# Giving the first weighted group of an attention + expert-mixture kernel the same matmul scheme as the others, with a new order where the scheme begins

## The chip, the cores and the metric

The kernel runs on one core of a Trainium2 chip. The metric is the device time of one execution in microseconds, as the median of several. Engines are named as in the profile: PE is TensorE, DVE VectorE, ACT ScalarE, POOL GpSimd, SP SyncE, which here only issues DMAs.

## The reference

Two blocks follow one another. The first is attention with a polynomial sketch in place of the softmax, for 4 x 4 heads of 1088 positions and 32 dimensions. Its output, read as 4352 rows of 128, is `x` of the second, a mixture of eight experts in which every expert sees every row and a Sinkhorn iteration gives the weights:

```python
logits = x @ w_gate                      # x: 4352 x 128, w_gate: 128 x 8
P = np.exp(logits - logits.max())
for _ in range(8):
    P /= P.sum(1, keepdims=True) + 1e-09
    P /= P.sum(0, keepdims=True) + 1e-09
    P *= N / E
for e in range(E):                       # w1[e]: 128 x 1024, w2[e]: 1024 x 128
    out += P[:, e:e + 1] * (np.maximum(x @ w1[e], 0.0) @ w2[e])
```

All of it is float32. Since P is positive, P times relu(x w1) is relu of (P times x) w1, so a kernel may weigh x ahead of an expert, or an expert's sum after it.

## The kernel before

Everything lies transposed: the 4352 rows of x are columns of a tile `xT`, features on the partitions. The expert part is a list of **groups**, each a range of columns with a number of tiles and a list of experts. An **item** is a group with one of its experts. An item's 1024 hidden features are eight slices of 128, and a **block** is half an item (four slices, in groups of three tiles of 256 columns) or a quarter (two slices, in groups of two tiles). A block has **first products**, x times W1, which ACT turns into hidden values by relu, and **second products**, hidden values times W2, which add up over the item or the group in four PSUM banks.

The routing weights are known only after the attention, so the list begins with **plain** groups (last field False): experts 0 and 1 on chosen columns, with unweighted x. Their sums are kept (`kept`) and weighed later. After them come five weighted groups of 768 columns, the first of them (`PLAIN`, columns 1280 to 2047) with experts 1 to 7, and at the end a weighted group of two tiles (columns 0 to 511) with experts 2 to 7. Plain groups run between the pieces of attention and routing.

The second products use fewer multiplications than the plain ones: seven for eight (`seven`) in groups of two tiles, twenty for twenty-four (`twenty`) in groups of three. For that, sums and differences of hidden values are made on DVE (`two`, `sum_of_four`), and sums and differences of W2 (the ten pieces of `make_four` on DVE and two on ACT, kept in DRAM by `store_four` for later groups).

The first products exist in two forms. The **old scheme** (`four`) multiplies as usual: per block 16 matmuls of 128 rows by 64 columns of the array, eight over 512 and eight over 256 columns of x. The **new scheme** (`middle`) has seven products, M1 to M7, in place of eight for a pair of slices, each two matmuls of 64 by 64 over 384 columns, 28 matmuls in a block; a block has two pairs, e and o. It needs W1 in two prepared forms (`forms_ahead`: loads, sign changes on ACT and adding DMAs on POOL's queue, results `wl` and `wf` in DRAM), x in two halves, weighed on DVE (`weigh_half`), copied on ACT (`copy_half`) and joined by four adding DMAs on POOL's queue (`join_halves`), and for each pair six copies and relus and a DVE addition ahead of M3 and one after M7. In that scheme also the second products are split by rows into 64 by 64 matmuls.

All engine orders are written out by hand. In plain groups, and in the old scheme, a loop in `steps` emits a first product, then what is due at that step; second products follow eight steps behind (`LAG`). In the new scheme each operation has a time within a period of 8.83 us, and all operations are sorted by these times and emitted in that order; the times fix only the order. DMAs that `keep_in_program_order` holds stand in their queue (SP's or POOL's) where the program puts them.

The new scheme begins with `first_new`, the third item of the first weighted group, expert 3:

```python
first_weighted = next(j for j, (g, e) in enumerate(items) if g == PLAIN)
first_new = first_weighted + 2
```

Experts 1 and 2 of that group run in the old scheme, with x weighed by POOL (`weigh`) or DVE (`weigh_by_vector`) and with raw W1. During their 32 steps, `beside` and `PREPARE` also make these experts' forms of W2, the W1 forms of expert 1, and the joined x of expert 3. At the seam to the new scheme, the second products of the last two old blocks fill TensorE while the first new blocks start. Routing ends with a transpose on DVE, four DMAs of the weights to `pT` in DRAM, all on SP's queue, and loads of a row of `pT`, repeated over all partitions, to `px`.

Of the kernel before, what the change touches and what calls it, by code (L numbers as in the profile page):

```python
# [10 lines left out]
F32 = mybir.dt.float32  # L11
# [7 lines left out]
def f64_to_f32(nc, pool, raw, shape):  # L19
# [5 lines left out]
    def u32(name):  # L25
        return pool.tile([p, n], U32, name=name)

    def f32(name):
        return pool.tile([p, n], F32, name=name)

    mant, top, expo, rest = u32("mant"), u32("top"), u32("expo"), u32("rest")
    out, inside, over = f32("s12"), f32("inside"), f32("over")
# [18 lines left out]
def kernel(  # L51
# [278 lines left out]

    def projections():
        flat = raw.rearrange("p n d -> p (n d)")
        s12 = f64_to_f32(nc, consts, flat, (P, 2 * D)) if words == 2 else flat.bitcast(F32)
        st = consts.tile([P, 2, 32], F32, name="st")
# [312 lines left out]
    def routing():  # L647
# [4 lines left out]
        for i, e in enumerate(range(items[first_new][1], E)):  # L652
# [46 lines left out]
        for b in (1, 0, 2, 3):  # L699
            nc.sync.dma_start(out=pT[:, b * S:(b + 1) * S],  # L700
                                                  in_=lgT[32 * b:32 * b + E].rearrange("p a s -> p (a s)"))
# [13 lines left out]
              (512, 384, 2, [1], False)]  # L715
# [24 lines left out]
    def prepare_w(j):  # L740
        g, e = items[j]
        three = groups[g][2] == 3
# [5 lines left out]
        else:  # L748
            loaded_w[j] = load_w(e, not three)
            if not three:  # L750
                ws, own = loaded_w[j][2]
                loaded_w[j] = *loaded_w[j][0:2], ws
                sums_ahead[j] = [lambda: weigh_by_vector(j, slice(0, 512)), *own]
        if three:
            loaded_w[j] = *loaded_w[j][0:2], sums_of_four(e)
# [7 lines left out]
    def first_weights(j):  # L763
        e = items[j][1]
        loaded_w[j] = []
        for t, tag in zip(fast[e], ("w1", "w2")):
            w = wpool.tile([P, F], F32, tag=tag, name=tag)
            tc.keep_in_program_order(nc.sync.dma_start(out=w, in_=t))
            loaded_w[j].append(w)
# [6 lines left out]
    def raw_second(j, tag):  # L776
        raw_w2[j] = wpool.tile([P, FO, DM], F32, tag=tag, name=tag)
# [15 lines left out]
    def weigh(out, x, pb):  # L793
        tc.keep_in_program_order(nc.gpsimd.tensor_tensor(out, x, pb, op=Alu.mult))

    def prepare_x(j):
# [5 lines left out]
        else:  # L802
            xe = weights_of(e, lo, t * n, "px")
            for sl in (slice(0, 512), slice(512, 768)) if j == first_weighted else ():
                weigh(xe[:, sl], x[:, sl], xe[:, sl])
            sources[j] = xe
# [36 lines left out]
    first_new = first_weighted + 2  # L843
# [3 lines left out]
    def weigh_kept(g, i, at_, add):  # L847
# [3 lines left out]
        pb = spare[:, (6 + 3 * (i % 2)) * NT3:][:, 0:n * t]  # L851
# [35 lines left out]
    def part(g, k):  # L887
# [4 lines left out]
        elif groups[g][2] == 3:  # L892
# [91 lines left out]
    def evacuate(k):  # L984
        g = ended.pop(k)
        part_of_twenty(g, k)
# [76 lines left out]
    LAG = 8  # L1063
# [4 lines left out]
    def room_of(k):  # L1068
# [8 lines left out]
        one, other = (13 * NT3 + size * ((k + 1) % 3), size * (k % 2)) if weighted else (size * (k % 3), size * (3 + k % 2))  # L1077

        def at(c):
            return base[:, c:c + size].rearrange("p (b n) -> p b n", b=4)[:, :, 0:n]  # L1080
# [58 lines left out]

    def four(k):  # L1140
        j, q = blocks[k]
        h = hs[k] = room_of(k)
        order = ((0, 0), (3, 0), (3, 1), (0, 1), (1, 0), (2, 0), (1, 1), (2, 1))

        def step(c):
            f, last = order[c]
            if last:
                first(k, 4 * q + PLACE[f], 2 * NT3, 3 * NT3, h[:, at(f, 2)], False)
            else:
                first(k, 4 * q + PLACE[f], 0, 2 * NT3, h[:, at(f, 0):at(f, 2)], False)  # L1150

        def sums(c):
            for i in {2: (0,), 3: (1,), 4: (2,), 6: (3, 4), 7: (7, 5), 8: (6,), 9: (8, 9)}.get(c, ()):
                sum_of_four(k, *SUMS[i][1:])

        return 8, step, sums
# [105 lines left out]
    def middle():  # L1262
# [21 lines left out]
        def first_product(k, p, n):  # L1284
# [3 lines left out]
            fa, fb = P * (4 * q + p), P * (4 * q + p + 2)  # L1288
            issued.append(n)
# [3 lines left out]
                      3: (by, 1, w1, fb, de[:, 0], False, True), 4: (b, 1, wf, fb, xe[:, 1], False, True),  # L1293
                      5: (b, p, wf, fa, de[:, 1], True, False), 6: (b, 0, wf, fb, de[:, 0], False, True),
# [20 lines left out]
        def vector(k, p, what):  # L1315
# [7 lines left out]
                  (17.63, 17.59, 19.18, 21.80, 21.41, 23.38, 23.73, 22.41, 24.54, 24.29))  # L1323
        EMPTY = 20.23, 24.2, 24.3, 29.0
        EASE, WEIGH = (11.93, 16.87, 13.85), 13.49

        def whole_product(k, i):
            if k not in products:
                products[k] = twenty(k)
            for p_ in products[k][i]:  # L1330
                into(items[blocks[k][0]][0], *p_)
                written.update({(p_[2], row): -1 for row in range(2)})
# [398 lines left out]
```

## Time and profile before

| | |
|---|---|
| time, median of 3 runs | 888.86 us (888.22 to 889.25) |
| the profiled execution | 889.38 us |
| its span in the profile | 887.6 us |
| PE, DVE, ACT, POOL busy | 99%, 88%, 63%, 19% |
| granted TensorE clock, mean | 0.998 |
| chain that ended last | PE 91%, DVE 4%, DMA 3%, issue 1%, ACT 1% |

All marks in time below are microseconds from the start of the span. A float32 matmul is recorded as two instructions, which overlap with their neighbours; so a record's duration is longer than what it adds to the chain, and costs are better read from the distance of marks and the number of records between. In the lines, `128*64` is the part of the array that a matmul uses, and `x4` the number of instructions merged in a line.

### The profile page before, as it was taken

To read this page: it belongs to the slowest core of one execution; us is meant where nothing else is said; L and a number is where in the kernel's file an instruction comes from. 1 tells how busy PE (TensorE), PEld (TensorE's weight loads), DVE (VectorE), ACT (ScalarE), POOL (GpSimd) and SP (SyncE) were. 2 spreads that over 40 slices of the span, in tenths; PEclk is the share of its full clock that TensorE was granted. 3 is DMA by queue.
4 is the path that set the end of the run, shared out by engine and by line. 5 is a ranking of instruction groups with operands and counts; after the bars stand their busy time and mean duration, and the time that the engine had idled before them with its cause. 6 is when DMAs were issued, how large, how long until landed. Compare 5 with 4: busy or idle time off the path is not lost.

```text
span 887.6 us, 28218 instructions
## 1 busy us (share of the span) xinstructions
PE 876.5 (99%) x11586; PEld 627.7 (71%) x11586; DVE 783.7 (88%) x1603; ACT 559.6 (63%) x1283; POOL 169.6 (19%) x234
## 2 busy tenths in 40 slices
PE   8999999999999999999999999999999999999997
PEld 6777644556677777777777777778778787766665
DVE  7678788989799999999999998999999999987865
ACT  3446377666576776676767666767667666655543
POOL 3121123012131123112222211321122212101000
PEclk9999999999999999999999999999999999999999
DMA  9996349668988879766895678767676975562340
GB/s 241 307 280 233 108 94 216 147 158 190 309 241 229 222 218 247 228 192 169 230 254 162 176 174 270 198 181 210 200 194 184 247 219 157 164 183 47 116 102 13
DMA packets 94881, 171.10 MB, mean 193 GB/s; under 512 B 28944, under 2 KB 67168, under 8 KB 89904
## 3 DMA queue, kind: packets, MB, share of 16 engines
q1 hardware_dynamic: 73264, 137.68, 50.0%
q0 software_dynamic: 20256, 31.45, 20.4%
q8 instruction: 91, 1.49, 0.7%
q10 hardware_dynamic: 1232, 0.16, 0.1%
q14 instruction: 38, 0.31, 0.1%
HBM read 123.60 MB, written 25.08 MB: 168 GB/s over the span
## 4 chain that ended last, share of the span: by engine, by line
PE 91%; DVE 4%; DMA 3%; issue 1%; ACT 1%; SPq 0%; DVEq 0%; POOLq 0%; ACTq 0%
PE s L1492 39%; PE a L1279 34%; PE a L1095 13%; DMA ph<-in_moe_w_dram 1%; PE a L423 1%; DVE hb L1181 1%; DMA kp<-in_moe_w_dram 1%; PE a L538 1%; DMA kx<-in_k_dram 1%; PE a L390 0%; PE s L452 0%; DVE hx L1181 0%; DVE ws L244 0%; DVE hb L1114 0%; PE a L502 0%
## 5 line engine op out<-in xcount | busy, mean ns | idle before, releaser
L1279 PE MATMUL a<-xe,w 64*64 64x384 f32 x2052 | 396.1, 483 | 0.0
L1492 PE MATMUL s<-hb,ws 64*64 64x256 f32 (+4 forms) x2904 | 376.4, 384 | 1.8 <-DVE hb L1114 0.9
L1492 PE MATMUL s<-hx,ws 64*64 64x256 f32 (+1 forms) x2844 | 349.5, 377 | 0.0
L1279 PE MATMUL a<-de,w 64*64 64x384 f32 x1536 | 296.7, 483 | 0.0
L1492 PEld LDWEIGHTS s<-hb,ws 64*64 64x64 f32 (+1 forms) x2904 | 199.4, 134 | 76.1 <-issue 26.3
L1492 PEld LDWEIGHTS s<-hx,ws 64*64 64x64 f32 (+1 forms) x2844 | 195.3, 134 | 57.0 <-issue 11.9
L1181 DVE TENSOR_TENSOR hb<-hb 128x512 f32<-128x512 f32 (+1 forms) x340 | 187.4, 576 | 3.4 <-ACT hb L1311 2.2
L1279 PEld LDWEIGHTS a<-xe,w 64*64 64x64 f32 x2052 | 139.7, 133 | 21.4 <-issue 3.4
L1311 ACT ACTIVATE hx<-a 128x384 f32<-128x384 f32 x192 | 90.8, 492 | 61.7 <-PE a L1279 60.2
L1311 ACT ACTIVATE hb<-a 128x384 f32<-128x384 f32 x192 | 91.8, 492 | 56.8 <-PE a L1279 55.1
L1279 PEld LDWEIGHTS a<-de,w 64*64 64x64 f32 x1536 | 106.6, 133 | 18.1 <-issue 0.8
L1095 PE MATMUL a<-xT,w 128*64 128x416 f32 (+3 forms) x512 | 119.2, 463 | 0.0
L1181 DVE TENSOR_TENSOR hx<-hx 128x512 f32<-128x512 f32 (+1 forms) x204 | 118.3, 593 | 0.2
L840 POOL DMA_DIRECT2D de<-xe x64 | 53.6, 992 | 280.9 <-ACT de L833 135.1
L1099 ACT ACTIVATE hb<-a 128x256 f32<-128x256 f32 (+4 forms) x152 | 68.8, 462 | 60.3 <-PE a L1095 52.6
L1095 PE MATMUL a<-px,w 128*64 128x256 f32 (+1 forms) x512 | 93.6, 407 | 0.0
L1307 ACT ACTIVATE hb<-a 128x384 f32<-128x384 f32 x128 | 62.8, 490 | 33.4 <-PE a L1279 32.5
L1316 DVE TENSOR_TENSOR a<-a,hb 128x384 f32<-128x384 f32 x128 | 72.0, 563 | 10.1 <-PE a L1279 7.9
L1305 ACT COPY a<-a 128x384 f32<-128x384 f32 x128 | 59.3, 463 | 30.5 <-PE a L1279 30.2
L1114 DVE TENSOR_TENSOR hb<-hb 128x416 f32<-128x416 f32 (+7 forms) x84 | 58.5, 697 | 19.6 <-ACT hb L1099 15.9
L1099 ACT ACTIVATE hx<-a 128x256 f32<-128x256 f32 (+1 forms) x104 | 41.6, 400 | 42.1 <-PE a L1095 35.0
L1095 PEld LDWEIGHTS a<-xT,w 128*64 128x64 f32 x512 | 48.9, 137 | 25.4 <-issue 14.5
(216 smaller groups left out, 1022.2 us busy)
## 6 DMA issues: line engine op xcount, KB each, us to landing
ws<-ws SPq DMA_DIRECT2D x34, 1280.0 KB, 6.4
w<-wl SPq DMA_DIRECT2D x32, 512.0 KB, 7.8
w<-wf SPq DMA_DIRECT2D x32, 512.0 KB, 8.9
px<-pT SPq DMA_DIRECT2D x34, 384.0 KB, 9.4
w<-in_moe_w_dram SPq DMA_DIRECT2D x18, 512.0 KB, 4.4
de<-xe POOLq DMA_DIRECT2D x32, 192.0 KB, 3.6
de<-de POOLq DMA_DIRECT2D x32, 192.0 KB, 8.1
ph<-qa SPq DMA_DIRECT2D x12, 288.0 KB, 5.0
```

Source lines behind the costliest of these rows:

```text
L423: nc.tensor.matmul(pv[64 * s:64 * (s + 1), i], kp[0:n, H * t + h].rearrange("p i j -> p (i j)"), vx[0:n, slots[h], t, :], start=(t == 0 an ...
L840: tc.keep_in_program_order(nc.gpsimd.dma_start(out=out, in_=x, accum_op=Alu.add))
L1095: nc.tensor.matmul(ph[sl], loaded_w[j][0][:, P * f + H2 * s:P * f + H2 * (s + 1)], sources[j][:, lo:hi], start=True, stop=True, tile_posit ...
L1099: last_relu[:] = [nc.scalar.activation(out=out, in_=ph, func=Act.Relu).ins.name]
L1114: nc.vector.tensor_tensor(out, a, b, op=Alu.subtract)
L1181: nc.vector.tensor_tensor(places(out), places(a), places(b), op=Alu.subtract if off else Alu.add)
L1279: nc.tensor.matmul(out[sl], w[r, c0 + H2 * s:c0 + H2 * (s + 1)], x[r], start=start, stop=stop, tile_position=(H2 * row, H2 * s), skip_grou ...
L1305: witness(k, p, 1, nc.scalar.copy(b, bx))
L1307: witness(k, p, 5, nc.scalar.activation(out=m5s[p], in_=b, func=Act.Copy, scale=1.0 if p else -1.0))
L1311: ins = nc.scalar.activation(out=out, in_=x, func=Act.Relu)
L1316: ins = nc.vector.tensor_tensor(by if what == 1 else raw(k, p, 1, 1), bb[p], m5s[p], op=Alu.add)
L1492: mm = nc.tensor.matmul(sums[g][i][H2 * s:H2 * (s + 1), n * place:n * (place + 1)], w, x, start=c == (2 if t == 3 and row is None else 1) ...
```

## The change

Every item of the weighted groups of 768 columns uses the new scheme: `first_new` is `first_weighted`. With that go these parts.

- Expert 2 on columns 0 to 511 moves from the last group to a plain group of its own ahead of the weighted ones. Its sum goes to a third kept tile, `kept2`, which lies where the conversion of S1 and S2 had its tiles, and is weighed late in the new scheme.
- This item's four blocks issue only their first products ahead of the seam. Their second products (`held_blocks`, `seven`) are emitted inside the new scheme's order, in 14 places, between the first blocks' products.
- The first four blocks of the new scheme, and the evacuations, sums, forms and second products around them, take their times from a table, `SEAM`, and not from the period.
- W1 forms are made ahead, during routing, for experts 1 to 5, and inside the new scheme for 6 and 7. Forms of W2 are made for expert 1 at the seam and for 2 to 7 in the six items after it.
- Of the four DMAs that write `pT`, that of columns 1088 to 2175 stays on SP's queue, and the other three go to POOL's.
- In the last steps before the seam (`TAIL`), DVE weighs x for the first two items, ACT copies and POOL joins them; raw W2 of expert 1 goes to a buffer of forms that is still free (`ws4`), and its second W1 form to two free buffers of output sums (`y`), in halves.

The diff, cut to its core:

```diff
-        for i, e in enumerate(range(items[first_new][1], E)):
+        for i, e in enumerate(range(1, 1 + AHEAD)):
...
         for b in (1, 0, 2, 3):
-            nc.sync.dma_start(out=pT[:, b * S:(b + 1) * S],
-                                                  in_=lgT[32 * b:32 * b + E].rearrange("p a s -> p (a s)"))
+            tc.keep_in_program_order((nc.gpsimd if b != 1 else nc.sync).dma_start(
+                out=pT[:, b * S:(b + 1) * S], in_=lgT[32 * b:32 * b + E].rearrange("p a s -> p (a s)")))
...
-              (512, 384, 2, [1], False)]
+              (512, 384, 2, [1], False), (0, 256, 2, [2], False)]
...
-    groups.append((0, 256, 2, list(range(2, E)), True))
+    groups.append((0, 256, 2, list(range(3, E)), True))
...
-    kept = [keep.tile([P, N], F32, name="kept0"), keep.tile([P, 1280], F32, name="kept1")]
+    kept = [keep.tile([P, N], F32, name="kept0"), keep.tile([P, 1280], F32, name="kept1"), kept2]
...
+    def first_second_forms(j):
+        halves = [pools[0].tile([P, 3, NT3], F32, tag="y", name="y").rearrange("p t n -> p (t n)")[:, 0:F // 2]
+                  for _ in range(2)]
+        for h, x in zip(halves, (fast[items[j][1]][1][:, F // 2 * i:F // 2 * (i + 1)] for i in range(2))):
+            tc.keep_in_program_order(nc.sync.dma_start(out=h, in_=x))
+        second_forms[j] = halves
...
     def raw_second(j, tag):
-        raw_w2[j] = wpool.tile([P, FO, DM], F32, tag=tag, name=tag)
+        if tag == "ws4":
+            ws = pools[0].tile([P, len(FORMS), FO // 4, H2], F32, tag=tag, name=tag)
+            raw_w2[j] = ws.rearrange("p n q d -> p (n q d)")[:, 0:FO * DM].rearrange("p (f d) -> p f d", f=FO)
+        else:
+            raw_w2[j] = wpool.tile([P, FO, DM], F32, tag=tag, name=tag)
...
-    first_new = first_weighted + 2
+    first_new = first_weighted
+    held_blocks = range(4 * first_new - 4, 4 * first_new)
...
-        elif groups[g][2] == 3:
+        elif groups[g][2] == 3 or PLAIN - 2 <= g < PLAIN:
             ended[k] = g
...
+        SEAM = {"x2a": (0.199,), "x2b": (1.073,), "E2": (2.951,), "E3": (3.623,), "L1": (5.253,), "L2": (8.499,),
...
+                "M1e": (-0.125, 6.079, 17.849, 24.101,), "M2e": (1.111, 10.224, 18.41, 28.325,),
...
+        def when(name, n, usual):
+            own = SEAM.get(name, ())
+            return own[n] if 0 <= n < len(own) and own[n] is not None else n * PERIOD + usual
...
-                    add(t + at_[p], first_product, k, p, name)
+                    add(when(f"M{name}{'eo'[p]}", n, at_[p]), first_product, k, p, name)
...
-        for i in (2, 3, 4):
-            add(0.01 * i, second_product, ks[0] - 2, i, 1)
-            add(6.5 + 0.2 * i, second_product, ks[0] - 2, i, 0)
-        for i, at_ in ((0, 1.5), (1, 1.6), (5, 3), (6, 4.5), (7, 5.5), (8, 7.3), (9, 7.6)):
-            add(at_, whole_product, ks[0] - 2, i)
-        for row in range(2):
-            for i, at_ in enumerate(SECOND[row]):
-                add(at_ - PERIOD, second_product, ks[0] - 1, i, row)
+        fillers = [seven(k) for k in held_blocks]
+        fillers = [ps for f in fillers for ps in f[:3]] + [fillers[i][3] + fillers[i + 1][3] for i in (0, 2)]
+        for name, ps in zip(FILL, fillers):
+            add(SEAM[name][0], whole_products, ps)
+        for name, i in (("E2", 2), ("E3", 3)):
+            add(SEAM[name][0], evacuate, i)
...
+    AHEAD = 5
...
+    TAIL = {12: ((weigh_half, first_new, 0), (raw_second, first_new, "ws4")), 13: ((copy_half, first_new, 0),),
+            14: ((weigh_half, first_new, 1), (first_second_forms, first_new)), 15: ((copy_half, first_new, 1),),
+            16: ((join_halves, first_new), (first_weights, first_new)), 18: ((weigh_half, first_new + 1, 0),),
+            20: ((weigh_half, first_new + 1, 1),), 21: ((evacuate, 0),), 23: ((evacuate, 1),)}
...
-        prepare_x(PLAIN)
+        fetch_weights(first_new)
+        fetch_weights(first_new + 1)
```

More of the change, by code (lines that the diff above doesn't have):

```diff
@@ L16, with f64_to_f32 @@
 PSUM = bass.MemoryType.PSUM
-def f64_to_f32(nc, pool, raw, shape):
+def f64_to_f32(nc, room, raw, shape):
     p, n = shape
     low, high = raw[:, 0::2], raw[:, 1::2]
[L25 to L32, printed above, removed]
+    out, inside, over, *words = (room[:, n * i:n * (i + 1)] for i in range(7))
+    mant, top, expo, rest = (w.bitcast(U32) for w in words)
     shift_right, shift_left = Alu.logical_shift_right, Alu.logical_shift_left
@@ L1138, in at @@
         return 13 + 3 * f + t
[L1140 to L1156, printed above, removed]
     pqg = spare[:, 0:3 * NT3].rearrange("p (b n) -> p b n", n=NT3)
@@ L1587, in steps @@
                     loaded_w.update({i: w for i in loaded_w if items[i][1] == items[j + 1][1]})
-                m, step, sums_ = ready.get(k) or (four if tiles == 3 else two)(k)
-                products = old_twenty if tiles == 3 else eight if g in DIRECT else seven
+                m, step, sums_ = ready.get(k) or two(k)
+                products = eight if g in DIRECT else seven
             for c in range(m if k < len(blocks) else 4):
@@ L1608, in steps @@
                         later.pop(0)()
-                elif later and (tiles == 3 or c % 2 or share > 0.9):
+                elif later and (c % 2 or share > 0.9 or c and weighted):
                     later.pop(0)()
```

197 lines of the change are left out of this document (99 added, 98 removed), and 37 rows, old and new, of the table SEAM.

## Prediction, made before the changed kernel ran

> **What bounds the kernel now.** I read the page first, then the waits of TensorE, then busy time by stage.
>
> ```profile
> span 887.6 us, 28218 instructions
> PE 876.5 (99%) x11586; PEld 627.7 (71%) x11586; DVE 783.7 (88%) x1603; ACT 559.6 (63%) x1283; POOL 169.6 (19%) x234
> ...
> PE 91%; DVE 4%; DMA 3%; issue 1%; ACT 1%; SPq 0%; DVEq 0%; POOLq 0%; ACTq 0%
> ...
> PE s L1492 <- DVE hb L1114: 0.9, 2, 0.7
> PE s L1492 <- DVE hb L1181: 0.6, 1, 0.6
> ```
>
> TensorE is busy for 99% and makes up 91% of the chain that ended last; its longest waits on VectorE are under a microsecond each. So the end moves with what is queued on TensorE, unless another engine can't feed it. The stages say where that is:
>
> ```profile
> core 0: us, PE busy (x) PEld busy (x) DVE busy (x) ACT busy (x) POOL busy (x), PEclk, DMA share, GB/s
> 186.77:221.29 34.52, 34.52 (x240) 21.65 (x236) 31.10 (x70) 23.68 (x53) 8.05 (x9) 1.00 0.68 153
> 221.29:237.71 16.42, 16.42 (x188) 9.37 (x190) 10.63 (x25) 7.49 (x19) 1.73 (x2) 1.00 1.04 308
> 246.60:309.47 62.87, 62.63 (x966) 45.91 (x962) 62.75 (x146) 44.80 (x103) 13.75 (x16) 1.00 0.87 237
> 398.87:487.18 88.31, 88.31 (x1364) 69.42 (x1360) 84.83 (x176) 60.83 (x139) 19.47 (x24) 1.00 0.75 205
> 826.69:839.64 12.95, 12.95 (x122) 8.63 (x120) 10.35 (x24) 6.14 (x16) 0.00 (x0) 1.00 0.32 102
> ```
>
> Row one is the old scheme for experts 1 and 2, row two the seam to the new scheme, row three its blocks 2 to 8, in which VectorE also makes the forms of W2. Row four is ten later blocks, row five one item of the last group.
>
> The fourth row gives TensorE's price. A new block has 28 first matmuls of 384 columns and 40 second ones of 256, each recorded twice: 56 x 384 + 80 x 256 = 41,984 columns of quarter-array work in 8.83 us, 0.2103 ns each. It holds for the last group: 120 records x 256 columns x 2 (half-array) at that price are 12.92 us, and the row says 12.95.
>
> In the third row VectorE is busy for 62.75 of 62.87 us. Seven blocks at TensorE's own pace would be 61.8. So this stage, and no other, goes at VectorE's pace: 0.433 us for each of its instructions there (62.87 / 145).
>
> **The change, part by part.**
>
> *Four blocks of first products.* An old block has 16 matmuls, 8 of 512 and 8 of 256 columns, on half the array: 24,576 quarter columns, 5.17 us. A new one has 28 x 2 x 384 = 21,504, 4.52 us. Four blocks save 4 x 0.65 = 2.6 us of TensorE. The 20 second products are the same arithmetic. The rest of the account asks whether the seam and VectorE let that through, so I lay the changed kernel out in time, from the last point that both share, and compare it at a point where both are in the same state.
>
> *From 186.77 to the seam.* Up to 186.77 us the engines' compute orders are the same. The first matmul of the old scheme stood there; now the plain item for expert 2 does. Its first products are 64 of an item's 120 records, 12.95 x 64 / 120 = 6.9 us; its second products are held back as filling. Beside them run the 14 left-over second matmuls of the item before, 28 x 384 x 2 x 0.2103 = 4.5 us. The new scheme starts at 186.77 + 11.4 = 198.2. ACT has 21 copies and relus in these 11.4 us at 0.435 each (44.80 / 103), 9.1 us, so it keeps up.
>
> *The seam itself.* The order of the built kernel shows, from there to product M6 of the second block, 18 first products and 26 of the held half-array matmuls: 36 x 2 x 384 x 0.2103 = 5.8 and 52 x 512 x 0.2103 = 5.6 us, 11.4 together. The held matmuls stand in six clusters among the quarter-array ones. What such a cluster costs is seen in the old seam:
>
> ```profile
> 224.82 0.54 PE L1279 MATMUL a<-de,w 64*64 64x384 f32 x2
> ...
> 226.04 0.65 PE L1492 MATMUL s<-hx,ws 128*64 128x256 f32 x4
> 226.63 0.54 PE L1279 MATMUL a<-de,w 64*64 64x384 f32 x2
> ...
> 227.43 0.65 PE L1492 MATMUL s<-hx,ws 128*64 128x256 f32 x4
> 228.01 0.54 PE L1279 MATMUL a<-de,w 64*64 64x384 f32 x2
> ```
>
> From 226.04 to 228.01 are 1.97 us for eight half-array records and eight records of 384 columns between them, worth 0.86 + 0.65 = 1.51: 0.23 us lost for each of two clusters. [...] Six clusters lose 1.4 us. About 0.7 us more goes where a product on one half of the rows has no partner on the other: three of the first four products use the lower rows. So M6 of block 1 starts at 198.2 + 11.4 + 2.1 = 211.7. The old seam was no better: its 16.42 us (row two above) held 78 records of 384 and 80 of 256 columns, and 28 half-array ones of 256, worth 13.6 us: 2.8 lost.
>
> ```profile
> L1279 PE MATMUL a<-xe,w 64*64 64x384 f32 x44 | 9.0, 499 | 0.0
> L1279 PE MATMUL a<-de,w 64*64 64x384 f32 x34 | 6.6, 491 | 0.0
> L1492 PE MATMUL s<-hb,ws 64*64 64x256 f32 x52 | 6.2, 378 | 0.0
> L1492 PE MATMUL s<-hx,ws 128*64 128x256 f32 x28 | 3.9, 394 | 0.0
> L1492 PE MATMUL s<-hx,ws 64*64 64x256 f32 x28 | 3.6, 380 | 0.0
> ```
>
> *VectorE's stage gets longer.* Forms of W2 are made for experts 1 to 7 now, so it runs from block 1 to block 13 and not from about 2 to 9. These are VectorE's marks, its first addition of a block (block 0, 2 and 9):
>
> ```profile
> 225.80 0.57 DVE L1316 TENSOR_TENSOR a<-a,hb 128x384 f32<-128x384 f32 x1 [0.29 <-PE a L1279]
> ...
> 246.61 0.56 DVE L1316 TENSOR_TENSOR a<-a,hb 128x384 f32<-128x384 f32 x1
> ...
> 309.47 0.55 DVE L1316 TENSOR_TENSOR a<-a,hb 128x384 f32<-128x384 f32 x1
> ```
>
> The first came 1.0 us after M6 had started (224.82), so in the changed kernel VectorE's mark of block 1 is at 212.7. From it to that of block 13 its order holds 248 instructions: 119 sums, 48 additions in the first products, 60 pieces of forms, 12 weighings, 3 of a kept sum and 6 of the evacuated plain group. At 0.433 they take 107.5 us; TensorE's own work between the same marks, 334 matmuls of 384 and 466 of 256 columns (two of them half-array), is 104.3 by its price, so VectorE decides. The mark of block 13 comes at 320.2. In between TensorE is held up some 2.5 us, where it was 0.6 before: the longer stage gives back most of the saving, and only the cheaper seam is left.
>
> *From there to the end.* Block 13 now and block 9 before stand in the same place, the second half of expert 7 in the first weighted group, with 54 new blocks behind them. Before, 887.6 - 309.47 = 578.1 us were left. One item of the last group is gone (expert 2, made plain ahead of the seam), 12.95 us, as TensorE is dense there. 320.2 + 565.2 = 885.4, 2.2 us less than the span; I take 2.0, for small waits in the new order of ACT, which has 41 instructions, 17.8 us, in the 19.7 us from the seam to block 2.
>
> *Edits that cost nothing.* Forms of W1 are made for five experts during routing as before, and for two beside the new scheme as before (then one in the old scheme, one in the new); only which experts changes. The weighing of expert 2's kept sum adds two pieces of VectorE and a load and an add by DMA late in the new scheme, where VectorE idles 3.5 us in ten blocks (row four); without that room they would cost 0.8 us. `kept2` reuses the room of the conversion of S1 and S2. Raw W2 of expert 1 and the two halves of its second W1 form are loaded before the seam, behind the routing weights on SP's queue; behind them stands only W1 itself, which waits for TensorE's last use of its buffer (just before 186.77) and has until 198.
>
> *Routing's result.* The weights pT were written by four DMAs on SP. Now one goes by SP and three by POOL's queue, and the built order has the load of px wait for all four.
>
> ```profile
> 172.50 1.31 DVE L698 STREAM_TRANSPOSE qT<-kT 128x1088 f32<-128x1088 f32 x1
> 173.84 1.33 SPq L700 DMA_DIRECT2D pT<-qT  x4
> 177.15 0.82 SPq L790 DMA_DIRECT2D px<-pT  x2
> 184.39 2.33 POOL L794 TENSOR_TENSOR px<-xT,px 128x512 f32<-128x512 f32 x2 [19.79 <-DMA wl<-in_moe_w_dram]
> 204.87 1.66 POOL L840 DMA_DIRECT2D de<-xe  x2 [7.95 <-ACT hb L1099]
> 214.99 0.88 POOL L840 DMA_DIRECT2D de<-de  x1 [8.45 <-DMA de<-xe]
> ...
> de<-xe POOLq DMA_DIRECT2D x32, 192.0 KB, 3.6
> de<-de POOLq DMA_DIRECT2D x32, 192.0 KB, 8.1
> ```
>
> px was issued 2.0 us after SP had issued the last write (173.84 + 1.33), and was there by 184.39. POOL issues two DMAs in 1.66 us, so its third is out near 176.4; landing as fast as SP's, px goes out near 178.4, with two loads fewer ahead of it. VectorE's first weighing now stands at about 184.0 in its order, and four sums and the next first product's relu are queued behind it; I give this edit nothing, and the bounds below.
>
> **Profile and median.** The profiled execution took 889.38 us, its span 887.6, 1.8 around it. 885.6 + 1.8 = 887.4 for such an execution; it lay 0.5 above the median of 888.86, so I forecast a median of 886.8. A difference of 0.2% is 1.8 us, about what a measurement of this kernel can tell from none.
>
> **The rivals.**
>
> *VectorE doesn't decide.* If the forms squeeze into TensorE's pace, the 2.5 us of holding up are not there, and only seam and products count: 884.4. For it: the ten later blocks run at 8.83 with VectorE 96% busy. Against it: 62.75 of 62.87. Chance 0.13.
>
> *The halves aren't joined in time.* M5 of block 0 needs the first pair of adding DMAs, M6 the next, at 198.5 and about 201 (three products on the lower rows, 2.0 us, and a cluster, 0.7). They can start at 188: the first weighing at 184.0, then two sums, an addition and the second weighing on VectorE, and a relu and a copy on ACT, nine instructions of some 0.45. By the rows, the pair took until 214.99 - 204.87 = 10.1 us after its start and de<-de lands a median of 8.1 after that; its shortest possible, 3.6 + 0.9 + 3.6, would be 8. So it is ready between 196 and 206, against 201, and TensorE's queue stands behind M6 for 0 to 5 us. At 2 us, the middle of what is late, the saving is gone: 888.8. Chance 0.25, as SP's queue is quiet from about 195 until TensorE frees the next buffer.
>
> *Routing's result is late.* This is the one that ends slower. If POOL's writes land like its slower DMAs, 8.1 and not 2.0 us after issue, px goes out at 184 and lands near 191. VectorE then stands at the first weighing, seven microseconds late; join and seam move with it, and the filling of the seam doesn't help, as its sums are queued behind. The plain work hides some 2 us; the rest, about 5, is paid: 891.8. It decides once px is issued later than about 180. [...] Chance 0.15.
>
> That the change doesn't do what it says I leave out: the built order has 1,906 matmuls of the new first kind where there were 1,794, four blocks of 28 more.
>
> **How the numbers follow.** The forecast, VectorE's pace with a seam that loses about 2 us, gets 0.47: 886.8, of its own 885.5 to 888.3. The range of all reaches from 884.6 (VectorE not deciding) to 890.5, which takes in the late join up to 3.5 us and the mild half of late weights. Faster by over 0.2% means under 887.1: most of the first rival and somewhat over three quarters of the forecast, 0.51. Within 0.2% are the rest of it and most of the late join, 0.34. Slower by over 0.2%, above 890.6, are the late weights and the worst of the joins, 0.15.
>
> **What would show it.** Right: TensorE's first product of the new scheme near 198, block 1's first VectorE addition near 213, VectorE without idle time from there until about 320, and then 8.83 us a block. Wrong in the seam: TensorE waiting there for de<-de, or for ACT. Wrong in the weights: px landing after 185 and VectorE idle before its first weighing. If VectorE shows idle time in blocks 3 to 12 while TensorE is dense, the stage price was wrong.

## The result: slower, by 6 us

| kernel | median, us | against the kernel before, 95% interval |
|---|---|---|
| before | 888.88 | |
| changed | 895.03 (893.48 to 898.83) | 1.0071 (1.0059 to 1.0084) |

The forecast was 886.8, and its range ended at 890.5. The profiled execution of the changed kernel is the slowest of its six, 898.83 us, 3.8 above the median; a second profile, of an execution of 896.14, is among the experiments.

The page of the changed kernel:

```profile
span 897.0 us, 28696 instructions
PE 880.0 (98%) x11790; PEld 640.2 (71%) x11790; DVE 792.7 (88%) x1628; ACT 572.1 (64%) x1312; POOL 176.5 (20%) x244
...
PE 92%; DMA 4%; DVE 2%; ACT 1%; issue 0%; SPq 0%; POOL 0%; DVEq 0%; ACTq 0%
```

The waits of TensorE (who waited, for whom, us in total, times, longest), the largest first:

```profile
PE a L1279 <- DMA w<-wf: 3.9, 1, 3.9
PE a L1279 <- ACT a L1308: 2.2, 1, 2.2
PE a L1279 <- DVE hb L1319: 1.4, 1, 1.4
```

Before, no wait of TensorE in the expert part reached 1 us. Now there are three single ones. The first two stand in the stage where the prediction looked at VectorE alone: TensorE waits there for a second form of W1 (`wf`) on its way from DRAM, and for ACT. Busy time by stage, in the columns shown for before; the marks are the start of the new scheme and VectorE's first additions of blocks 1, 2, 13 and 23:

```profile
186.77:198.85 12.08, 12.08 (x96) 8.15 (x92) 9.49 (x20) 8.26 (x21) 3.43 (x4) 1.00 0.82 201
198.85:213.72 14.87, 14.87 (x131) 6.07 (x132) 11.72 (x27) 11.85 (x29) 3.38 (x4) 1.00 0.86 253
213.72:224.10 10.38, 8.96 (x116) 5.40 (x114) 9.36 (x23) 8.55 (x21) 1.11 (x1) 1.00 0.53 112
224.10:332.34 108.24, 101.87 (x1508) 76.87 (x1506) 99.28 (x228) 71.34 (x165) 25.22 (x29) 0.98 0.85 227
332.34:420.52 88.18, 88.18 (x1363) 73.05 (x1358) 83.23 (x170) 61.24 (x139) 20.47 (x24) 1.00 0.79 224
```

The last row, ten blocks in 88.18 us, is the old pace. The fourth is where the time went: TensorE is idle for 6.4 us there, and VectorE, which was to be busy throughout, for 9.

To compare kernels I keep an account of TensorE's lost time: the distance between two marks, less the work recorded between them at 0.2083 ns for each column of quarter-array work. That is a unit of account, not a measured speed: I set it 1% under the 0.2103 ns that the prediction takes from ten dense blocks, so ten such blocks lose 0.8 us in it. The last 5 us of a span, behind TensorE's last product, are not in the table. In the kernel before, the second row takes in the old scheme's stage.

| lost by TensorE, us | before | changed | no forms beside (e2) | forms of 7 earlier (e4) |
|---|---|---|---|---|
| to 186.77 | 17.5 | 17.4 | 17.1 | 17.7 |
| to block 2 of the new scheme (seam) | 4.1 | 6.3 | 5.9 | 6.2 |
| to block 9 (before) or 13 | 1.3 | 11.8 | 2.9 | 3.1 |
| from there to TensorE's last product | 10.7 | 10.7 | 10.8 | 11.3 |
| work | 848.5 | 846.0 | 846.0 | 846.0 |

The work fell by 2.5 us, as forecast, and the rest of the program runs as before. The seam lost 2.2 us more, and the stage after it 10.5.

What happened in that stage is one chain, which the timeline of the changed kernel shows (start, duration, engine, line, out<-in; in brackets the idle time before, and what ended it):

```profile
270.73 1.65 POOL L842 DMA_DIRECT2D de<-xe  x2 [10.36 <-ACT de L835]
280.42 0.89 POOL L842 DMA_DIRECT2D de<-de  x1 [8.04 <-DMA de<-xe]
281.53 2.74 POOL L276 DMA_DIRECT2D forms<-in_moe_w_dram  x2
287.37 0.63 ACT L282 ACTIVATE forms<-forms 64x512 f32<-64x512 f32 x1 [3.19 <-DMA forms<-in_moe_w_dram]
289.37 0.54 PE L1279 MATMUL a<-de,w 64*64 64x384 f32 x2 [2.18 <-ACT a L1308]
...
302.42 0.88 POOL L842 DMA_DIRECT2D de<-de  x1 [9.17 <-DMA de<-xe]
303.52 1.54 POOL L276 DMA_DIRECT2D forms<-forms  x1
308.15 0.53 SPq L279 DMA_DIRECT2D wf<-forms  x1
...
310.70 0.32 SPq L770 DMA_DIRECT2D w<-wf  x1
...
317.74 0.54 PE L1279 MATMUL a<-de,w 64*64 64x384 f32 x2 [3.95 <-DMA w<-wf]
```

These are the W1 forms of expert 7. Their adding DMAs stand on POOL's queue behind the join of an item's x, and the join stands 8.0 and then 9.2 us for its own first half. So ACT's next sign change waits 3.19 us for the forms, the copies queued behind it are late, and TensorE waits 2.18 us for those. One join later the last addition goes out at 303.52, the store at 308.15, the load of the finished form at 310.70, and TensorE, which needs it from 313.8 on, gets it at 317.74.

### The profile page after: what moved, and what is told of

It reads as the page before. It is cut to its first block, busy times and chain, and to the rows that moved or that the text cites. A ratio compares the mean times of both kernels' runs of the same rounds, so it can differ in the third digit from the quotient of the medians.

```text
span 897.0 us, 28696 instructions
## 1 busy us (share of the span) xinstructions
PE 880.0 (98%) x11790; PEld 640.2 (71%) x11790; DVE 792.7 (88%) x1628; ACT 572.1 (64%) x1312; POOL 176.5 (20%) x244
## 4 chain that ended last, share of the span: by engine, by line
PE 92%; DMA 4%; DVE 2%; ACT 1%; issue 0%; SPq 0%; POOL 0%; DVEq 0%; ACTq 0%
PE s L1546 41%; PE a L1279 36%; PE a L1113 12%; DMA kx<-in_k_dram 1%; PE a L419 1%; DMA w<-wf 1%; PE a L534 1%; DMA forms<-in_moe_w_dram 1%; DMA v<-in_v_dram 1%; DMA w<-wl 1%; DVE hb L1132 0%; PE a L386 0%; ACT hb L1314 0%; PE a L498 0%; DVE hb L1181 0%
## 5 line engine op out<-in xcount | busy, mean ns | idle before, releaser
L1279 PE MATMUL a<-xe,w 64*64 64x384 f32 x2164 | 419.7, 485 | 0.0
L1546 PE MATMUL s<-hb,ws 64*64 64x256 f32 (+4 forms) x2962 | 382.7, 384 | 1.8 <-DVE hb L1132 0.9
L1279 PE MATMUL a<-de,w 64*64 64x384 f32 x1600 | 305.9, 483 | 6.1 <-DMA w<-wf 3.9
L1546 PEld LDWEIGHTS s<-hb,ws 64*64 64x64 f32 (+1 forms) x2962 | 207.0, 133 | 72.9 <-issue 23.1
L1279 PEld LDWEIGHTS a<-xe,w 64*64 64x64 f32 x2164 | 147.3, 133 | 18.3 <-ACT hx L1314 1.7
L1314 ACT ACTIVATE hb<-a 128x384 f32<-128x384 f32 x204 | 97.6, 492 | 57.6 <-PE a L1279 56.0
L1113 PE MATMUL a<-xT,w 128*64 128x256 f32 (+3 forms) x576 | 130.1, 454 | 0.0
L1117 ACT ACTIVATE hb<-a 128x256 f32<-128x256 f32 (+3 forms) x148 | 66.5, 453 | 62.6 <-PE a L1113 53.2
L1310 ACT ACTIVATE hb<-a 128x384 f32<-128x384 f32 x136 | 66.7, 490 | 35.4 <-PE a L1279 34.2
L1546 PE MATMUL s<-hb,w 128*64 128x256 f32 (+3 forms) x280 | 69.8, 435 | 0.0
L842 POOL DMA_DIRECT2D de<-de x34 | 30.0, 883 | 144.1 <-DMA de<-xe 72.5
```

Of the source, the lines that this page charges most:

```text
L842: tc.keep_in_program_order(nc.gpsimd.dma_start(out=out, in_=x, accum_op=Alu.add))
L1113: nc.tensor.matmul(ph[sl], loaded_w[j][0][:, P * f + H2 * s:P * f + H2 * (s + 1)], sources[j][:, lo:hi], start=True, stop=True, tile_posit ...
L1117: last_relu[:] = [nc.scalar.activation(out=out, in_=ph, func=Act.Relu).ins.name]
L1279: nc.tensor.matmul(out[sl], w[r, c0 + H2 * s:c0 + H2 * (s + 1)], x[r], start=start, stop=stop, tile_position=(H2 * row, H2 * s), skip_grou ...
L1310: witness(k, p, 5, nc.scalar.activation(out=m5s[p], in_=b, func=Act.Copy, scale=1.0 if p else -1.0))
L1314: ins = nc.scalar.activation(out=out, in_=x, func=Act.Relu)
```

## The experiments

| | kernel | median, us | against before |
|---|---|---|---|
| e1 | changed, once more | 895.37 | 1.0069 (1.0053 to 1.0086) |
| e2 | no W1 forms beside the new scheme | 889.64 | 1.0000 (0.9991 to 1.0010) |
| e3 | e2, and no forms of W2 | 888.64 | 0.9994 (0.9985 to 1.0003) |
| e4 | forms of expert 7 earlier | 891.24 | 1.0023 (1.0013 to 1.0033) |
| e5 | six sets of forms in routing | 891.97 | 1.0040 (1.0025 to 1.0054) |
| e6 | e5, two times of the seam moved | 891.39 | 1.0027 (1.0016 to 1.0038) |
| e7 | e4, two times of the seam moved | 890.70 | 1.0019 (1.0009 to 1.0028) |
| e8 | e4, pT by SP alone | 891.41 | 1.0025 (1.0015 to 1.0035) |
| e9 | e7, additions later | 893.88 | 1.0060 (1.0039 to 1.0081) |
| e10 | e9, two clusters fewer | 895.13 | 1.0071 (1.0045 to 1.0097) |
| e11 | e7, additions on POOL | 894.20 | 1.0059 (1.0047 to 1.0071) |
| e12 | before, without W1 forms beside | 889.06 | 1.0001 (0.9992 to 1.0010) |

A ratio stands against runs of the kernel before from the same session, and need not be the quotient of two medians here. Where two intervals overlap, as those of e2 and e3, of e4 to e8 and of e9 to e11, the medians alone do not tell the two kernels apart. A profile is of one execution: those of e9, e10 and e11 are each the fastest of six, 1.8, 4.1 and 1.9 us under the median. In the edits below, `...` stands for what is left out.

**e1: the changed kernel, profiled again.**

> The changed kernel unchanged, for a second profile, since the first was of an execution 3.8 us above the median of 895.0. Theory A (the W1 forms of experts 6 and 7, made beside the new scheme, come too late): TensorE waits again at the same two places, near 289 us for ACT and near 317 us for w<-wf, but for shorter in sum, 2 to 5 us instead of 6.1; median 894 to 896. Theory B (VectorE's pace in the stage with the forms of W2 is the main loss): those two waits are accidents of the first profile, absent here, and the lost time is spread evenly over blocks 2 to 13.

The same waits at the same two places: 2.4 us for ACT and 2.4 for `w<-wf`. In the account block 8 to 9 loses 3.3 us and block 11 to 12 4.4 (3.1 and 5.9 in the first profile), while the other blocks behind block 4 lose 0.5 or less. This is theory A's outcome.

**e2: no forms beside.**

```diff
-        for e, times in ((6, (10, 15.43, ...)), (7, (3 * t + 5, ...))):
-            ...                              # forms_beside(e), nine steps each
+        for e in (6, 7):
+            fast[e] = fast[5]
```

> The W1 forms of experts 6 and 7 are not made; their items load those of expert 5 (the output of these two experts is therefore another). VectorE's work is unchanged; ACT loses 8 sign changes, POOL 6 adding DMAs, SP 16 transfers. Theory A: the account of TensorE's lost time between 279 and 332 us in the first profile is 9.8 us where six blocks at VectorE's pace cost about 2.5, so 7.2 us go from the 898.8 of that execution: 891 to 892. Theory B: nothing on VectorE changes, so the time stays within 1 us of 895: 894 to 895.5.

889.64: 5.4 to 5.7 us less than the changed kernel, more than theory A asked for, and theory B is out. TensorE waits at neither place, and the ratio to before is 1.0000. By itself this run does not tell the lateness of the forms from the work of making them, since both are gone; e4 and e12 do.

**e3: no forms of W2 either.**

```diff
-                        add(t + 15.72, make_second, j + 1)
-                        for i, at_ in enumerate((16.87, 22.68, ...)):
-                            add(t + at_ + 1e-3 * i, lambda j=j, i=i: forms_w2[j + 1][i]())
+                        add(t + 15.72, lambda j=j: loaded_w[j + 1].append(loaded_w[first_new][2]))
```

> As the kernel without forms beside the new scheme, and besides the forms of W2 of experts 2 to 7 are not made in the first weighted group: their items use those of expert 1 (raw W2 is still loaded, the forms are still stored). VectorE loses 60 instructions less the 10 of expert 1, ACT 12 copies. The prediction had 2.5 us of TensorE's time lost to VectorE's pace in these blocks: by theory A with that, 2 to 3 us below the kernel without forms beside, 888.5 to 890. By theory B all of the loss beyond the seam goes here, 5 us or more below it. If VectorE's pace costs nothing: equal within 0.7 us.

888.64, within theory A's range as a number. But theory A asked for 2 to 3 us below e2, and the last reading for at most 0.7; it is 1.0, with overlapping intervals, and so between the two. The row from block 1's mark to block 13's, first of e2, then of e3:

```profile
213.41:322.76 109.35, 108.10 (x1618) 77.61 (x1620) 108.03 (x248) 75.75 (x176) 20.28 (x24) 1.00 0.74 203
```

```profile
212.72:320.58 107.86, 106.85 (x1611) 82.33 (x1613) 93.98 (x188) 71.97 (x164) 20.27 (x24) 1.00 0.76 221
```

VectorE did 248 instructions in e2, as counted in the prediction, at 0.436 us each, and was busy for 108.03 of 109.35. Yet with 60 fewer, and 13.9 us of idle time, the stretch is only 1.5 us shorter. Of that, 0.4 is the mark itself: TensorE has 7 records fewer behind it at block 13 (x1611 against x1618). In the account TensorE gained 1.1, which fits the medians. Relieving an engine that is 99% busy was worth about 1 us.

**e4: the forms of expert 7 earlier.**

```diff
-                         (7, (3 * t + 5, 3 * t + 15.43, 3 * t + 20.13, 4 * t + 6.6, 4 * t + 11.3, 4 * t + 12, 4 * t + 14.5,
-                              4 * t + 13.5, 5 * t + 6))):
+                         (7, (2 * t + 14.1, 3 * t + 9.4, 3 * t + 13, 4 * t + 6.6, 4 * t + 11.3, 4 * t + 12, 4 * t + 14,
+                              4 * t + 13.5, 5 * t + 2))):
```

> The whole computation; only the times of expert 7's W1 forms are moved: its loads stand right behind the last store of expert 6's (one half-item earlier, by 8.7 us), its two sign changes and adding DMAs ahead of POOL's join of the next item instead of behind it, and the last addition ahead of the following join. Theory A: ACT's wait for forms<-in_moe_w_dram and TensorE's wait for w<-wf at the first use of expert 7 go, so as without forms beside, 891 to 892.5. If the lateness comes from crowded DMA queues and not from the order: 894 to 896, with the same two waits.

891.24, in theory A's range: 3.8 to 4.1 of the 5.4 to 5.7 us come back from times alone, with all forms made. POOL's queue in the timeline of e4:

```profile
266.62 1.11 POOL L276 DMA_DIRECT2D forms<-in_moe_w_dram  x1 [7.17 <-ACT forms L282]
270.97 0.94 POOL L276 DMA_DIRECT2D forms<-in_moe_w_dram  x1 [3.24 <-PE a L1279]
271.59 2.01 POOL L842 DMA_DIRECT2D de<-xe  x2
283.73 0.89 POOL L842 DMA_DIRECT2D de<-de  x1 [10.13 <-DMA de<-xe]
```

The additions now go out ahead of the join, in time in which POOL stood idle. The join itself takes longer than before (10.13 us), so the queues are no emptier. It was when the forms are begun and what stands ahead of them that cost; e4 moves both and does not part them. Of the remaining 1.6 us to e2 a part is seen: ACT's first sign change of expert 6 stands in the seam (0.4 more lost there); the rest is open.

**e5 and e6: six sets in routing.** `AHEAD = 6`, five steps apart instead of six; e6 adds the change of e7.

> The whole computation; W1 forms of experts 1 to 6 are made during routing, an expert every five steps instead of six, and only those of 7 beside the new scheme, from the second item on (loads 27.7 us after its start instead of 58). Theory A: no wait for forms, as without forms beside (889.6), plus at most 1 us for the sixth set: 889.5 to 890.7. Rival: routing's end has no room for a sixth set, whose stores stand on SP's queue ahead of px: the first product of the new scheme comes 2 to 4 us later than 198.9, and the time is 892 to 894.

> As the kernel with six sets of forms in routing, and in the seam's table two times are moved: M4 of the second pair of block 1 from 17.9 to 18.2, behind six second products, and the emission of the plain group's four waiting additions on VectorE from 17.413 to 17.7, behind the addition that M4 waits for. TensorE lost 1.34 to 1.67 us at this M4 in every profile so far (1.0 to 1.4 named as a wait for VectorE's addition). If the order causes it: 1.0 to 1.6 less than the kernel with six sets alone. If VectorE is simply full there (its additions are only moved, none removed): the same wait a little later, equal within 0.5.

891.97 and 891.39: e5 stands at the lower edge of the rival's time and above theory A's. No wait for forms remains. In the profiles of e5 and e6, 5.4 and 5.6 us are lost between 100 and 187 us, where e2 loses 4.2 and e4 3.9: the sixth set is paid in routing with 1.2 to 1.7 us. The rival's sign, a start 2 to 4 us later than 198.9, did not come: e5 starts at 199.4. Its profile is of an execution some 1.5 us under the median, so the rest of the 2.3 us to e2 is not seen. The seam's two times gave 0.6, within the intervals.

**e7: two times of the seam.**

```diff
-                "M4o": (8.152, 17.9, ...), "ls0": (None, 17.413, 34.276,)
+                "M4o": (8.152, 18.2, ...), "ls0": (None, 17.7, 34.276,)
```

> The kernel with expert 7's forms earlier (891.2), and the same two times of the seam's table moved. If the order causes the wait in the seam: 889.6 to 890.3. If VectorE is full there: 890.8 to 891.7.

890.70, 0.5 less than e4, between the two readings and not clear of noise. In the profiles, block 1 to 2 loses 1.8 us instead of 2.6, and block 2 to 3 1.0 instead of 0.5: most of the wait moved a block on, as the rival had it, and 0.25 us went. The additions on VectorE are not all of that wait: in the changed kernel VectorE stood 0.64 us idle among the four, for ACT.

**e8: pT by SP alone.** The writes are those of the kernel before.

> The kernel with expert 7's forms earlier (891.2), with all four writes of pT on SP's queue again, as in the kernel before. The prediction gave the two queues nothing, with routing's result late by up to 5 us as the rival. If the queues matter nothing: within 0.6 of 891.2, and the new scheme starts within 0.5 us of 198.9. If POOL's queue delays the weights: 1 us or more faster. If the two queues bring the weights earlier and that is needed: 1 to 2 us slower.

891.41 against 891.24; the load of px is issued at 177.85 us and the new scheme starts at 199.2, with the two queues of e4 at 177.84 and 198.95. No difference.

**e9 and e10: additions later, fewer clusters.** In e9 the additions of the evacuated plain group are issued one at a time in blocks 7 to 12, and expert 6's first two sign changes come 4 to 5 us later, its next steps 1.5 to 3. In e10 F3_2 moves from 7.6 to 9.5 and F1_1 from 10.373 to 10.0.

> The kernel with expert 7's forms earlier and the two seam times moved (890.7), and besides: the six additions on VectorE of the plain group evacuated at the seam are issued one at a time in blocks 7 to 12, not in blocks 1 to 3, and expert 6's two first sign changes come 5 us later, behind the seam. In the profiles the lost time from block 1's to block 3's mark is 2.85 us with the two times moved, against 3.1 with the table's own (0.5 in the same two blocks before). If VectorE's load at the seam is the cause: 1.3 to 2.0 less there, 888.8 to 889.5. If the loss is the order of TensorE's own products: within 0.5 of 890.7.

> As the kernel with the additions later, and two of the seven clusters of the held second products join their neighbours (the third of the last held block behind M4 of block 0, the second of the second block ahead of M2 of block 1). The prediction took 0.23 us for a cluster. If a change between half-array and quarter-array products costs that: 0.4 to 0.6 less than with the additions later alone, from the lost time between block 0's and block 1's mark (1.89 us in every profile). If the filling is missing where it stood: equal or slower by up to 0.5.

In the profile the seam became better, block 1 to 3 losing 1.75 instead of 2.85, and the kernel became worse: 893.88. The rows from block 7's mark to block 13's, of e4, of e7, on which e9 builds, and of e9:

```profile
270.20:323.80 53.60, 53.36 (x822) 38.45 (x816) 53.58 (x125) 38.03 (x88) 12.04 (x14) 1.00 0.88 254
```

```profile
269.50:324.90 55.40, 54.13 (x822) 37.63 (x818) 53.79 (x125) 38.16 (x88) 12.03 (x14) 1.00 0.87 253
```

```profile
267.20:324.80 57.60, 56.20 (x826) 37.29 (x822) 55.70 (x130) 38.48 (x89) 12.00 (x14) 1.00 0.84 244
```

Against e7, five VectorE instructions more are 1.9 us more busy time and 2.2 more in all. Waiting for px, whose load stands on SP's queue behind a store of expert 7's forms, takes 1.0 us of VectorE in e9 and 0.7 in e7, so it is not this edit's doing. But e4 and e7 have the same order in these blocks, and they differ by 1.8 us from one execution to another; in e4 VectorE had 0.02 us of idle time here, in e7 1.6. So the 2.2 us fit the reading that VectorE has no room here, and do not show it. The two profiles differ by 0.8 us in all, the medians by 3.2. What the slower executions lose, and how it divides between VectorE and expert 6's later forms, is open, since e9 changes both.

In the profile of e10, block 0 to 1 loses 2.2 us instead of 1.9, so two clusters fewer gained nothing there. No wait is named in that stretch; that the filling was missing where it had stood is the reading that is left, and is not shown. Nor is the price of 0.23 us for a cluster borne out.

**e11: the additions on POOL.** `nc.gpsimd.tensor_tensor` in place of `nc.vector.tensor_tensor`, in one row behind the third item's join.

> The kernel with expert 7's forms earlier and the two seam times moved (890.7); the six additions of the plain group evacuated at the seam are made by POOL, in one row behind the join of the third item (about 260 us), where POOL stood idle for 5.9 us, and not by VectorE. Putting them later on VectorE took 1.1 us from the seam and gave 2.7 back in blocks 8 to 13. If VectorE has no room anywhere from the seam to block 13, taking them off it keeps the 1.1 us: the lost time from block 1's to block 3's mark falls from 2.85 to about 1.7, blocks 8 to 13 stay as they were, and the time is 889.2 to 890.0. If the wide spread of the kernel with the additions later came from the joins, not from VectorE, POOL's six instructions (0.7 us each) make it wider: 891 to 893.

894.20, above both ranges. In the profile, block 1 to 3 keeps its gain (1.9 lost), and blocks 5 to 7 lose 3.9 us instead of 0.6; TensorE waits there once for 2.5 us, for an addition of VectorE. The groups of VectorE in the six microseconds of POOL's additions (busy us, mean ns), first of the changed kernel in the same stretch, then of e11:

```profile
L828 DVE TENSOR_TENSOR xe<-xT,px 128x384 f32<-128x384 f32 x1 | 0.6, 558 | 0.0
L1181 DVE TENSOR_TENSOR hx<-hb,hx 128x256 f32<-128x256 f32 x1 | 0.4, 420 | 0.0
```

```profile
L1189 DVE TENSOR_TENSOR hx<-hb,hx 128x256 f32<-128x256 f32 x1 | 2.1, 2053 | 0.0
L828 DVE TENSOR_TENSOR xe<-xT,px 128x384 f32<-128x384 f32 x1 | 1.1, 1080 | 0.0
```

The same two instructions took twice and five times as long while POOL added. Neither of the two readings had this: the additions left VectorE's queue, and VectorE's other instructions became longer instead. That accounts for the profiled execution; the median lies 1.9 us above it.

**e12: before, without forms beside.** As e2, with `fast[1]` and `fast[2]` set to `fast[3]`.

> The kernel before, without the two sets of W1 forms that it makes beside the old and the new scheme (experts 1 and 2; their later items use the forms of expert 3, so these experts' output is another). The counterpart of the changed kernel without forms beside (889.64, ratio 1.0000 with 0.9991 to 1.0010). In the kernel before, the first of them is used after block 10, some 100 us after it is begun. If forms made with time to spare cost nothing: within 0.5 of the kernel before, 888.5 to 889.4, and the new scheme by itself, with seam and VectorE's stage, gains nothing. If forms cost some 1 to 2 us even then (as the 1.6 us between the changed kernel with expert 7's forms earlier and without any suggest): 887.0 to 888.0, and the scheme by itself loses as much.

889.06 against 889.13, as the first reading had it. Forms that have time cost nothing that these runs can tell. With e2 this compares the two schemes without them: both stand at 1.000 to before, within 0.1%, so the scheme and its seam, apart from the forms, gain nothing measurable.

## Why the prediction was wrong, step by step

**The step that failed** is "edits that cost nothing": that two sets of W1 forms are made beside the new scheme as before, and "only which experts changes". When each is begun and due is the point. In the kernel before, the second set (expert 2) is loaded from 226 us on and first used by block 12's first product, at 331.9 us. In the changed kernel the old scheme's stage is gone, and both sets are made beside the new one; they share one tile, so that of expert 7 can't begin before expert 6's last store (254.2 us), is loaded from 264 on, and is due at 313.8, at the same product: 50 us where there were 106. The prediction counted the sets, and never wrote down these times; it priced them at nothing. The runs showed a cost of 5.4 to 5.7 us (e1 and the changed kernel against e2), of which 3.8 to 4.1 go with other times (e4), and nothing measurable in the kernel before, where the sets have time (e12).

**Four blocks of first products: right.** TensorE's work fell by 2.5 us (2.6 forecast).

**Up to the seam: right.** The new scheme starts at 198.85 (198.2); in the other profiles with five sets made ahead it starts between 197.5 and 199.2.

**The seam: its first half right, its second missing.** Block 1's mark came at 213.72 (212.7). Behind it lies a wait that I had not looked for: M4 of block 1 stands 0.9 us behind the M7 whose result VectorE must first add, and four additions of the evacuated plain group are queued ahead of that addition: 1.43 us of waiting, 2.6 lost from block 1 to 2. Before the seam, the prediction passed over a wait: TensorE's longest for VectorE was not under a microsecond but 2.1 us, in attention (`PE a L390 <- DVE kT L378: 2.1, 1, 2.1`). It lies in the part that both kernels share.

**VectorE's stage: the count right, the reasoning not.** Without the late forms (e2) there are 248 instructions, as counted, and the stage takes 109.35 us (107.5). But VectorE's pace was a small part of what held TensorE: with 60 instructions fewer TensorE gained about 1 us (e3), where the prediction's two terms have VectorE put 107.5 - 104.3 = 3.2 on top of TensorE's own time. (Its text says 2.5. And the trace has 337 matmuls of 384 and 471 of 256 columns between these marks, not 334 and 466: 105.3 us by its price.) What remains stands early: from block 1 to block 6 e3 still loses 3.4 us, 2.1 of them up to block 2, with the seam's wait. So that the stage's length came within 2% is in part luck: much of it is a wait that the prediction did not have.

**From block 13 to the end: right.** 564.9 us in e2, 564.7 in the changed kernel (565.2). So the sum without the forms misses by 2.8: 0.7 up to block 1, 1.85 from there to block 13, 0.6 in what lies between profile and median (889.64 - 887.7 = 1.94 in e2, 1.3 taken), and 0.1 because the forecast stands that much below its own sum (887.4 - 0.5 = 886.9), less 0.5 at the end (564.9 against 565.2 and the 0.2 taken for ACT).

**The rivals.** The halves were joined in time: the first pair of DMAs went out at 188.16 (188 forecast), the second at 196.04, and TensorE has no wait for either. Routing's result was not late (e8). That VectorE decides little is what e3 shows, but the saving of that rival did not come: e3 stands at 888.64, not at 884.4, and half of what it loses in the stage is lost up to block 2. The outcome was in none of them: slower, by a mechanism that stood in a list of free edits.

No version here is clearly faster than the kernel before; the nearest that leaves nothing out is e7, at 1.0019.

## What to carry to other kernels

When a change moves a group of work earlier, list for every product made on the side when it is due now, and in which in-order queue its steps stand: "made beside, as before" is a claim about due times and not about room. Here POOL's queue, kept in program order, held an instruction that waited 8.0 and then 9.2 us for another transfer, and the forms' transfers stood behind it; issuing them earlier and ahead of the waiting one brought back 4 us. And an engine that is nearly always busy need not be the bottleneck: take work off it before believing so. Here VectorE was busy for 108.03 of 109.35 us, and taking 60 of its 248 instructions away was worth about 1 us.

## What the runs showed of the hardware

**Behind two waits of TensorE the granted clock was 0.50 for 3.41 us.** In the clock records of before and of the first profile of the changed kernel, the stretches at full clock last 880.64 us (before), 314.03 and 573.44 us (changed). These are 258, 92 and 168 times 3.413, and the one stretch at half clock inside the changed kernel's work lasts 3.41. The rows here are cut at multiples of that length from its start (the granted clock stands behind POOL's column): three of the changed kernel around the wait of 3.95 us for `w<-wf`, then three of e1, the first with most of its wait of 2.39 us for ACT, the second with its wait of 2.43 us for `w<-wf`.

```profile
312.12:315.53 3.41, 1.67 (x29) 1.04 (x21) 3.41 (x9) 1.28 (x3) 0.00 (x0) 1.00 1.14 239
315.53:318.94 3.41, 1.20 (x18) 1.09 (x22) 0.53 (x3) 0.30 (x1) 0.36 (x1) 1.00 0.96 364
318.94:322.35 3.41, 3.41 (x32) 2.49 (x28) 1.14 (x3) 1.96 (x5) 1.38 (x2) 0.50 0.84 255
```

```profile
284.25:287.66 3.41, 1.56 (x24) 0.84 (x20) 2.93 (x9) 1.42 (x3) 0.00 (x0) 1.00 0.49 79
311.55:314.96 3.41, 0.98 (x18) 0.47 (x14) 3.12 (x9) 1.06 (x3) 0.00 (x0) 1.00 1.07 313
314.96:318.37 3.41, 3.41 (x28) 2.71 (x31) 0.00 (x0) 1.18 (x3) 0.00 (x0) 0.50 0.96 345
```

Behind the row with TensorE busy for 1.20 us the clock was 0.50, and behind the one with 0.98; behind those with 1.67 and 1.56 it was 1.00. Cut in this way throughout, the profile of before and that of the changed kernel have three stretches that half clock follows, with 1.20 us of TensorE and, at the program's end, 0.94 and 0.00; all others have at least 1.67. What sets the clock, they do not show. In e1 the wait for ACT, nearly as long as the other, runs across the end of a row at 287.66, and the clock stayed at 1.00; that its place made the difference is my reading, and no run moves a wait alone. The row at half clock has 32 records of TensorE, the 3.41 us after it 60. Half clock for 3.41 us is by that about 1.7 us of TensorE: with it the waits of 3.95 and 2.43 make 5.7 and 4.1, and the blocks lost 5.9 and 4.4.

**Instructions of VectorE took longer while POOL added.** The rows of e11 above: 420 ns became 2,053 and 558 became 1,080 in the stretch of POOL's six additions, which took 0.8 to 1.6 us each. An addition `a<-a,hb`, at 262.52 us beside the last of the six, took 552 ns, where the changed kernel's took 560. Which of the two engines waited, and for what, they do not show: the instruction of 2,053 ns stands from 256.88 us on, ahead of POOL's first addition at 257.23. Nor do they show whether POOL's additions were longer than without VectorE beside them. It is one execution.
